# A new table of half steps for the attention phase, sums of exponentials on VectorE for two more batches, and the preparation of w_in2 as one chain with rooms of its own

## The chip, the core and the metric

The kernel runs on one core of a Trainium2 chip. The metric is the device time of one execution in microseconds (us), the median of three runs. TensorE (PE, with its weight loads as PEld), VectorE (DVE), ScalarE (ACT) and SyncE (SP, which only issues DMAs here) each execute their own instructions strictly in the order of the program and wait for each other through semaphores.

## The reference

The inputs are `q`, `k`, `v` of shape (8 batches, 8 heads, 576 tokens, 64) and `phi` (8, 8, 576, 32) in fp32, and the weights of two MLPs, `w_in` (512 x 2048) and `w_out` (2048 x 512), in 64-bit floats.

```python
a = exp(phi - max over tokens); a = a / (sum over tokens + 1e-9)
k_m, v_m = einsum("bhsm,bhsd->bhmd", a, k), einsum("bhsm,bhsd->bhmd", a, v)    # 32 memory slots
scores = q @ k_m^T / sqrt(64); attn = softmax(scores)
x = heads joined (attn @ v_m)                                  # 4608 x 512
y = (s * relu(x @ w_in1) ** 2 + b) @ w_out1                    # first MLP
out = relu(y @ w_in2) ** 2 @ w_out2                            # second MLP
```

## The kernel before

**Arithmetic.** Weights arrive as 64-bit words; `narrow` turns them into fp32 with one ACT and three DVE instructions. Every fp32 operand of a large product is split into a rounded half (an ACT copy) and the remainder (a DVE subtraction), and three products of halves are added (`split3`). The first MLP's second product and both products of the second MLP are done by a scheme with seven products (`e` = 0 to 6) in place of eight, on sums and differences of the quarters of the operands.

**Four stages.** (1) Attention, with the first MLP's hidden layer: the eight batches are taken one after the other. For a batch, `front_max`, `front_t1`, `front_t2`, `front_less` and `front_exp` make the exponentials of phi; `kvs` sums keys and values over the tokens by 72 small matmuls in three groups `g`; it also needs the sum of the exponentials, either by 72 further small matmuls against a column of ones (batches 0 to 2), or by 8 after `front_sum` has added the nine token groups on DVE (batches 3 to 7). `kv_over`, `kv_norm`, `kv_turn` normalize and transpose; `q_turn`, `scores`, `q_exp`, `q_sum`, `p_turn` make the attention weights, in three groups; `fold` multiplies the values into a quarter of `w_in1` (four folds a batch); `hidden` multiplies attention weights with the folded weights. (2) The second product of the first MLP, six blocks of seven products, each in four parts of 12 matmuls of 384 columns. (3) and (4) The two products of the second MLP.

**Half steps.** The attention stage has 256 half steps (slots): batch, 16 blocks of 128 hidden columns, 2 halves of the tokens. Each ends with one `hidden`: six matmuls of 288 columns and an ACT instruction into a tile `r`. After every second slot a DMA writes `r` to DRAM (`rd`). All other work of the attention stage, for this batch and for the next ones, is hung on slots by hand (`on(slot, go, ...)`): it is issued just ahead of that slot's `hidden`. While the stage lasts (`Written.held`), every engine keeps exactly this order, SP's DMAs too. The fold, the scores and the transposes share three PSUM banks (`ps_m`).

**End of the attention stage.** From slot 192 on, and again from 224, `wo1_combos` prepares `w_out1` on ACT and DVE, two steps a slot. The tiles it reads are the four rooms `rc`, in which the first block's `r` is then loaded back (`quad`); the first items of that block (`BEGUN`: square, casts) run in the last slots.

**Second stage.** `block_ready` lists, for each product `e`, what must be ready: squares (ACT), differences (`less`, DVE), casts (`cast`, ACT and DVE, 128 x 768 elements each), and the loads (`quad`). The loop issues them four parts ahead of the matmuls. One step of `win` follows each part: the preparation of `w_in2`, by eight units `u`, 15 steps each: two raw halves are loaded, narrowed, summed, split, and written to DRAM (`wid`), in pairs. Raw halves and results share two rooms of 4 KB a partition (tag `t`).

## Time and profile before

| | us |
|---|---|
| median of three runs (1460.98 to 1464.67) | 1463.64 |
| the profiled execution, its own time | 1464.62 |
| its span, from the first to the last instruction | 1462.8 |
| up to the first `hidden` matmul | 37.1 |
| the 256 half steps | 341.8 |
| second stage (`ya`, `yb`, `yc`) | 362.9 |
| third stage (`pa`, `pb`, `pc`) | 352.3 |
| fourth stage (`qa`, `qb`, `qc`) to the end | 368.8 |

The stages are separated by the first matmul of each. The span leaves out 1.8 us of the execution's own time. In a row of the profile, "idle" is the time in which the engine did nothing before an instruction, and the name behind the arrow is what ended it; "issue" is a wait for nothing that the profile shows. PEclk is the clock that TensorE was granted, as a share of 2.4 GHz.

### The profile page before, as it was taken

The numbers are of one execution on the slowest core, as the hardware profiler recorded it, in microseconds if no ns is written. First come the engines' busy times: TensorE is split into PE (matmuls) and PEld (weight loads), VectorE is DVE, ScalarE is ACT, GpSimd is POOL, SyncE is SP. The second block draws the span as 40 slices with busy tenths as digits, with TensorE's granted clock in tenths as the row PEclk, the third lists the DMA queues.
The fourth block names the chain that finished last, engine by engine and source line by source line (L and its number), as shares of the span: only waits on it lengthen the run. The fifth ranks groups of instructions, "written<-read, shape, count | busy, mean of one in ns | idle before, by whom it ended". The sixth has DMA issues, their size and how long they took to land.

```text
span 1462.8 us, 28453 instructions
## 1 busy us (share of the span) xinstructions
PE 1416.8 (97%) x11616; PEld 1358.4 (93%) x11616; DVE 1068.2 (73%) x1545; ACT 797.6 (55%) x1403; POOL 1.2 (0%) x8
## 2 busy tenths in 40 slices
PE   5899999999899999999999999999999999999998
PEld 3787879878899999999999999999999999999998
DVE  5755777775789989887757786786756677776775
ACT  3555666666777777586535454554434443344443
POOL 0000000000000000000000000000000000000000
PEclk9999999999999999999999999999999999999999
DMA  9977988625574856754696665647796344433441
GB/s 294 285 239 234 291 280 262 220 106 190 173 253 150 306 197 217 234 172 156 231 359 228 246 237 181 247 172 260 277 351 250 113 145 145 143 114 112 138 145 30
DMA packets 207970, 306.47 MB, mean 210 GB/s; under 512 B 48224, under 2 KB 162912, under 8 KB 200288
## 3 DMA queue, kind: packets, MB, share of 16 engines
q1 hardware_dynamic: 207680, 304.39, 62.1%
q8 instruction: 91, 1.49, 0.4%
q14 instruction: 39, 0.32, 0.1%
q10 hardware_dynamic: 160, 0.26, 0.0%
HBM read 180.88 MB, written 123.73 MB: 208 GB/s over the span
## 4 chain that ended last, share of the span: by engine, by line
PE 73%; DVE 12%; DMA 8%; ACT 4%; issue 2%; SPq 1%; ACTq 0%; DVEq 0%
PE qa L109 14%; PE pa L107 13%; PE hps L109 11%; PE qc L109 7%; PE pc L107 7%; PE ya L831 4%; PE qb L109 4%; PE pb L107 3%; DVE rcast L107 3%; DMA wid<-wc 2%; PE yc L831 2%; PE vps L109 2%; PE kvs L109 2%; DMA wt<-in_moe_w_in_dram 2%; DVE wx L107 1%
## 5 line engine op out<-in xcount | busy, mean ns | idle before, releaser
L109 PEld LDWEIGHTS hps<-pt,vp 128*128 128x128 f32 x1536 | 210.4, 190 | 36.7 <-issue 18.3
L109 PE MATMUL hps<-pt,vp 128*128 128x288 f32 x1536 | 234.4, 304 | 6.5 <-ACT r L109 4.3
L109 ACT CAST gc<-h 128x1024 fp32r<-128x1024 f32 x119 | 123.2, 1048 | 174.2 <-DVE h L109 172.6
L109 PE MATMUL qa<-w,gc 128*128 128x256 f32 x1728 | 217.0, 283 | 1.0 <-DVE gc L109 0.7
L109 PEld LDWEIGHTS qa<-w,gc 128*128 128x128 f32 x1728 | 211.5, 192 | 1.6 <-DVE gc L109 1.0
L109 DVE TENSOR_TENSOR gc<-h,gc 128x1024 fp32r<-128x1024 f32 x119 | 145.5, 1224 | 89.0 <-ACT gc L109 89.0
L831 PE MATMUL ya<-rcast,w 128*128 128x384 f32 x1152 | 203.8, 337 | 2.9 <-ACT rcast L107 1.2
L107 PE MATMUL pa<-xc,w 128*128 128x384 f32 x1104 | 204.1, 337 | 0.0
L831 PEld LDWEIGHTS ya<-rcast,w 128*128 128x128 f32 x1152 | 199.8, 188 | 4.4 <-DVE rcast L107 2.1
L107 PEld LDWEIGHTS pa<-xc,w 128*128 128x128 f32 x1104 | 192.8, 188 | 0.6 <-DVE gr L107 0.2
L109 ACT ACTIVATE r<-hps 128x288 f32<-128x288 f32 x256 | 104.1, 416 | 70.0 <-PE hps L109 57.2
L831 PE MATMUL yc<-rcast,w 128*128 128x384 f32 x576 | 106.0, 344 | 5.3 <-DVE rcast L107 5.1
L109 PE MATMUL qc<-w,gc 128*128 128x256 f32 x864 | 109.5, 283 | 0.0
L831 PEld LDWEIGHTS yc<-rcast,w 128*128 128x128 f32 x576 | 103.0, 193 | 6.7 <-DVE rcast L107 6.0
L109 PEld LDWEIGHTS qc<-w,gc 128*128 128x128 f32 x864 | 106.3, 192 | 0.0
L107 PE MATMUL pc<-xc,w 128*128 128x384 f32 x552 | 104.0, 336 | 0.0
L107 PEld LDWEIGHTS pc<-xc,w 128*128 128x128 f32 x552 | 96.6, 188 | 0.3 <-DVE xc L806 0.3
L107 DVE TENSOR_TENSOR rcast<-r,rcast 128x768 fp32r<-128x768 f32 x92 | 84.7, 952 | 16.0 <-ACT rcast L107 16.0
L107 ACT CAST rcast<-r 128x768 fp32r<-128x768 f32 x92 | 73.8, 831 | 16.3 <-DVE r L107 8.5
L107 DVE TENSOR_TENSOR rcast<-rz,rcast 128x768 fp32r<-128x768 f32 x72 | 67.4, 953 | 19.8 <-ACT rcast L107 19.8
L107 ACT ACTIVATE gr<-pa 128x384 f32<-128x384 f32 x46 | 22.6, 492 | 101.1 <-PE pa L107 101.1
L107 DVE SCALAR_TENSOR_TENSOR gr<-gr 128x384 f32<-128x384 f32 x138 | 73.7, 552 | 1.9
(277 smaller groups left out, 1867.2 us busy)
## 6 DMA issues: line engine op xcount, KB each, us to landing
rd<-r SPq DMA_DIRECT2D x128, 288.0 KB, 3.7
gd<-gr SPq DMA_DIRECT2D x96, 384.0 KB, 3.6
h<-gd SPq DMA_DIRECT2D x34, 1024.0 KB, 5.4
wt<-in_moe_w_out_dram SPq DMA_DIRECT2D x16, 1024.0 KB, 6.9
r<-rd SPq DMA_DIRECT2D x16, 768.0 KB, 6.5
wid<-wc SPq DMA_DIRECT2D x24, 512.0 KB, 3.8
rz<-rd SPq DMA_DIRECT2D x16, 768.0 KB, 5.6
kv<-in_k_dram SPq DMA_DIRECT2D x24, 384.0 KB, 6.0
```

The costliest lines, as they stand in the source:

```text
L107: return go(*args, **kwargs)
L109: self.last = go(*args, **kwargs)
L831: nc.tensor.matmul(to[d], lhsT=w[:, wi, d], rhs=cast1[n, e, part][:, u, xi], start=(start and part == 0 and u == 0 and i == 0), stop=(part ...
```

## The change

1. All slots of the attention stage come from a table, `TABLE`, with one entry for each piece of work, in place of a few hand-written tuples and formulas. The start (`"begin"`) is another order too: loads and computing are mixed in it, phi of batch 0 is loaded and its maximum taken in four pieces, `w1_narrow(1, ...)` stands ahead of `kv_turn`, and the two small loads of `s` and `b` move to slots 152 and 153.
2. Batches 0 and 2 get their sum of exponentials from `front_sum`, as batches 3 to 7 do; batch 1 alone keeps the 72 small matmuls.
3. The loads of the first block of the second stage (`"qd"`) and its first items (`"bg"`) move by a few slots; its `b22` is loaded right at the opening of the second stage; in every block, `b12 - b22` and the load of `b21` move from product 4 to the end of product 3 in the list.
4. `prepare_in` takes the place of `combine_in`: one generator over all units, one raw half in the air at a time (one room), two rooms of 2 KB for results, a write to DRAM for each of the seven results (256 KB) in place of pairs (512 KB). A unit has 17 steps; a part takes 1, 0, 1, 2, 1, 1 or 1 of them, by its product.

```diff
+TABLE = {
+    "f": {1: [6, 9, 10, 12, 0], 2: [35, 37, 38, 40, 45], 3: [47, 51, 56, 57, 61], 4: [62, 64, 69, 69, 73], 5: [79, 84, 86, 89, 94], 6: [101, 109, 118,
+        121, 125], 7: [133, 140, 150, 150, 155]},
+    "pt": {1: [26, 30, 32], 2: [62, 63, 63], 3: [81, 87, 92], 4: [110, 115, 123], 5: [139, 148, 155], 6: [167, 176, 188], 7: [201, 208, 223]},
+    "qt": {1: [19, 20, 25], 2: [49, 52, 55], 3: [67, 68, 79], 4: [93, 97, 109], 5: [126, 136, 142], 6: [158, 164, 173], 7: [190, 197, 203]},
+    "kt": {1: 21, 2: 52, 3: 67, 4: 91, 5: 122, 6: 153, 7: 186},
+    "sc": {1: [22, 25, 26], 2: [53, 56, 59], 3: [68, 75, 84], 4: [99, 105, 113], 5: [128, 138, 144], 6: [160, 167, 178], 7: [192, 202, 207]},
+    "ks": {1: [15, 15, 16], 2: [46, 48, 48], 3: [62, 62, 63], 4: [81, 84, 85], 5: [96, 105, 114], 6: [128, 137, 146], 7: [160, 172, 178]},
+    "no": {1: [18, 18, 19], 2: [48, 50, 51], 3: [65, 65, 66], 4: [85, 87, 89], 5: [116, 118, 116], 6: [148, 150, 151], 7: [180, 182, 183]},
+    "ex": {1: [12, 13, 15], 2: [41, 40, 45], 3: [58, 60, 61], 4: [71, 72, 73], 5: [90, 90, 90], 6: [121, 122, 121], 7: [155, 155, 154]},
+    "qe": {1: [24, 27, 28], 2: [54, 58, 59], 3: [69, 80, 85], 4: [102, 107, 115], 5: [130, 138, 146], 6: [162, 171, 180], 7: [193, 204, 209]},
+    "qm": {1: [24, 27, 28], 2: [55, 58, 61], 3: [70, 80, 86], 4: [105, 107, 117], 5: [131, 139, 146], 6: [163, 171, 181], 7: [194, 204, 212]},
+    "fo": {0: [0, 8, 13, 23], 1: [30, 37, 46, 53], 2: [59, 71, 75, 81], 3: [85, 90, 99, 103], 4: [106, 113, 123, 128], 5: [137, 146, 155, 160], 6: [174,
+        178, 183, 191], 7: [199, 215, 212, 223]},
+    "wn": [[0, 0], [3, 3], [8, 9], [10, 11], [15, 16], [17, 18]],
+    "wl": [0, 3, 9, 10],
+    "lq": [1, 8, 4],
+    "lk": [12, 20, 31],
+    "lp": [14, 30],
+    "wo": [[64, 78, 78, 80, 81, 82], [83, 92, 96, 98, 99, 100], [98, 109, 109, 112, 113, 114], [109, 120, 122, 123, 123, 123], [124, 136, 136, 139, 141,
+        141], [138, 148, 151, 152, 153, 162], [152, 164, 167, 168, 171, 171], [164, 176, 178, 179, 185, 186]],
+    "sb": [152, 153],
+    "qd": [225, 227, 240, 244],
+    "begin": [("load_phi", 0), ("load_kv", 0, 2), ("w1_load", 0), ("load_kv", 0, 0), ("load_kv", 0, 1), ("w1_load", 1), ("load_q", 0, 0), ("load_q", 0,
+        1), ("load_q", 0, 2), ("load_phi", 1), ("w1_load", 2), ("front_max", 0), ("front_t1", 0), ("front_t2", 0), ("front_less", 0), ("w1_narrow", 0, 0),
+        ("front_exp", 0, 2), ("w1_load", 3), ("front_exp", 0, 0), ("front_exp", 0, 1), ("w1_narrow", 1, 0), ("kvs", 0, 0), ("front_sum", 0), ("load_kv", 1,
+        0), ("w1_narrow", 0, 1), ("kvs", 0, 1), ("kvs", 0, 2), ("kv_over", 0), ("load_kv", 1, 2), ("kv_norm", 0, 1), ("kv_norm", 0, 0), ("load_kv", 1, 1),
+        ("q_turn", 0, 0), ("w1_narrow", 1, 1), ("kv_turn", 0), ("q_turn", 0, 1), ("scores", 0, 0), ("q_exp", 0, 0), ("scores", 0, 1), ("q_turn", 0, 2),
+        ("q_exp", 0, 1), ("q_sum", 0, 0), ("scores", 0, 2), ("q_exp", 0, 2), ("q_sum", 0, 1), ("p_turn", 0, 0), ("q_sum", 0, 2), ("p_turn", 0, 1), ("fold", 0,
+        0), ("p_turn", 0, 2)],
+    "bg": [242, 245, 248, 250, 252, 253],
+}
...
-    def combine_in(u, pool):
-
-
-        src = w_in2.rearrange("(d p) (h f) -> d p h f", p=P, h=2)[:, :, :, u * P:u * P + P]
-        ts = []
-        for i in range(2):
-            ts.append(pool.tile([P, 1, 512], I64, tag="t", name="wt"))
+    def prepare_in(pool):
+
+
+        def load(u, i):
+            src = w_in2.rearrange("(d p) (h f) -> d p h f", p=P, h=2)[:, :, :, u * P:u * P + P]
+            raw = pool.tile([P, 1, 512], I64, tag="t", name="wt")
             for d in range(2):
-                sp.dma_start(ts[i][:, 0, d * 2 * P:d * 2 * P + 2 * P].rearrange("p (h c) -> p h c", h=2), src[2 * i + d])
-        yield
-        yield
-        x = wst.tile([P, 2, 512], I32, tag="x", name="wx")
-        for i in range(2):
-            for step, _ in enumerate(narrow(ts[i], None, x[:, i:i + 1])):
-                if step == 1:
+                sp.dma_start(raw[:, 0, d * 2 * P:d * 2 * P + 2 * P].rearrange("p (h c) -> p h c", h=2), src[2 * i + d])
+            return raw
+
+        t = load(0, 0)
+        for u in range(NU):
+            yield from (None,) * (3 if u == 0 else 1)
+            x = wst.tile([P, 2, 512], I32, tag="x", name="wx")
+            for i in range(2):
+                for step, _ in enumerate(narrow(t, None, x[:, i:i + 1])):
+                    if step == 0:
+                        yield
+                if i == 0:
+                    t = load(u, 1)
+                    yield from (None,) * 3
+                elif u + 1 < NU:
+                    t = load(u + 1, 0)
+            yield
+            a11, a12, a21, a22 = of_in(x.bitcast(F32))
+            sums_ = wst.tile([P, 4, 2, P], F32, tag="x", name="ws")
+            s1, s2, s4, s3 = [sums_[:, i] for i in range(4)]
+            for out, in0, in1, op in ((s1, a21, a22, ALU.add), (s2, s1, a11, ALU.subtract),
+                                      (s3, a11, a21, ALU.subtract), (s4, a12, s2, ALU.subtract)):
+                with behind():
+                    dve.tensor_tensor(out=out, in0=in0, in1=in1, op=op)
+            yield
+            for e, of in enumerate((a11, s1, s2, s4, s3, a12, a22)):
+                w = pool.tile([P, 2, 2, P], F32R, tag="wc", name="wc", bufs=2)
+                with behind():
+                    act.copy(w[:, 0], of)
+                    dve.tensor_tensor(out=w[:, 1], in0=of, in1=w[:, 0], op=ALU.subtract)
+                sp.dma_start(wid[u][:, e], w.bitcast(F32))
+                yield
+                if e in (1, 4):
                     yield
...
-            sp.dma_start(at["ph", b], pv[b])
+            for part in [slice(n, n + 1) for n in range(NP)] if b == 0 else [slice(NP)]:
+                sp.dma_start(at["ph", b][:, part], pv[b][:, part])
...
-        dve.tensor_reduce(out=pm.rearrange("p (n m) -> p n m", m=M),
-                                in_=at["ph", b].rearrange("p n j m -> p n m j"), axis=AX.X, op=ALU.max)
+        for part in [slice(n, n + 1) for n in range(NP)] if b == 0 else [slice(NP)]:
+            dve.tensor_reduce(out=pm.rearrange("p (n m) -> p n m", m=M)[:, part],
+                              in_=at["ph", b][:, part].rearrange("p n j m -> p n m j"), axis=AX.X, op=ALU.max)
...
-        summed = ([at["es", b]] if g == NJG - 1 else []) if b > 2 else [e[:, :, JG * g + j] for j in range(JG)]
+        summed = ([at["es", b]] if g == NJG - 1 else []) if b != 1 else [e[:, :, JG * g + j] for j in range(JG)]
...
-                if e == 2 and n == 0:
-                    put(None, quad, *b22)
                 if e in (0, 1, 2, 5):
                     put(None, square, (b11, b12, b22, None, None, b21)[e])
-                if e in (1, 2, 4, 6):
-                    put(None, less, *{1: (b11, b12, b11), 2: (b11, b22, b11), 4: (b12, b22, b12), 6: (b21, b21, b11)}[e])
-                if e == 4:
-                    put(None, quad, *b21)
+                if e in (1, 2, 6):
+                    put(None, less, *{1: (b11, b12, b11), 2: (b11, b22, b11), 6: (b21, b21, b11)}[e])
                 if e == 6:
                     put(None, quad, n + 1, "b12", half)
                 for part in (2 * half, 2 * half + 1):
                     put(4 * e + part, cast, e, part, (b11, b11, b11, b22, b12, b21, b21)[e])
+                if e == 3:
+                    put(None, less, b12, b22, b12)
+                    put(None, quad, *b21)
...
-    load_phi(0)
-    w1_load(0)
-    for g in range(NJG):
-        load_kv(0, g)
-    load_q(0, 0)
-    w1_load(1)
-    load_q(0, 1)
-    load_q(0, 2)
-    sp.dma_start(s_sb, s.rearrange("(o n) -> o n", o=1).to_broadcast([P, 1]))
-    sp.dma_start(b_sb, bb.rearrange("(o n) -> o n", o=1).to_broadcast([P, 1]))
-    w1_load(2)
-    w1_load(3)
-    load_phi(1)
-
-    for go, *args in [(front_max, 0), (front_t1, 0), (front_t2, 0), (front_less, 0), (w1_narrow, 0, 0),
-                      (front_exp, 0, 0), (front_exp, 0, 1), (front_exp, 0, 2), (w1_narrow, 0, 1), (kvs, 0, 0),
-                      (kvs, 0, 1), (kvs, 0, 2), (load_kv, 1, 0), (load_kv, 1, 1), (load_kv, 1, 2),
-                      (kv_over, 0), (kv_norm, 0, 0), (kv_norm, 0, 1), (kv_turn, 0),
-                      (q_turn, 0, 0), (scores, 0, 0), (w1_narrow, 1, 0), (q_turn, 0, 1), (q_exp, 0, 0), (w1_narrow, 1, 1),
-                      (scores, 0, 1), (q_turn, 0, 2), (q_exp, 0, 1), (scores, 0, 2), (q_sum, 0, 0), (q_exp, 0, 2),
-                      (q_sum, 0, 1), (p_turn, 0, 0), (q_sum, 0, 2), (p_turn, 0, 1), (fold, 0, 0), (p_turn, 0, 2)]:
-        go(*args)
+    FN = {f.__name__: f for f in (load_phi, w1_load, load_kv, load_q, front_max, front_t1, front_t2, front_less, w1_narrow, front_exp,
+          front_sum, kvs, kv_over, kv_norm, q_turn, kv_turn, scores, q_exp, q_sum, p_turn, fold, wo1_load, wo1_narrow, wo1_sum)}
+    for go, *args in TABLE["begin"]:
+        FN[go](*args)
...
-    fronts = {1: (6, 9, 11, 12, 0), 2: (34, 37, 39, 41, 0), 3: (47, 52, 54, 57, 62), 4: (66, 69, 71, 73, 78),
-              5: (79, 84, 86, 88, 92)}
-    sums_ = {1: (16, 17, 17, 18, 21), 2: (46, 47, 48, 49, 52), 3: (62, 63, 64, 65, 69), 4: (79, 82, 85, 86, 91)}
-    qs = {1: ((19, 20, 23), (22, 23, 25), (26, 28, 30)), 2: ((49, 52, 56), (53, 56, 58), (58, 61, 63)),
-          3: ((66, 68, 77), (73, 76, 82), (80, 86, 92))}
-    folds = {0: (0, 7, 15, 23), 1: (29, 39, 46, 54), 2: (61, 70, 76, 82), 3: (87, 97, 105, 114)}
...
-        y, z = SB * (b - 2), SB * (b - 1)
-        top, turn, back, less, whole = fronts.get(b, (y - 27, y - 18, y - 10, y - 9, y - 3))
-        *adds, norm, last = sums_.get(b, (y, y + 9, y + 18, y + 20, y + 26))
-        qt, sc, pt_ = qs.get(b, ((z - 2, z + 5, z + 13), (z, z + 9, z + 18), (z + 8, z + 17, z + 28)))
...
-            on(folds.get(b, (z + 9, z + 18, z + 26, z + 32))[n], fold, b, n)
...
-    for i, a in zip(range(2, 2 * NV), (0, 2, 8, 10, 15, 17)):
-        on(a, w1_narrow, i, 0)
-        on(a + 1, w1_narrow, i, 1)
...
-        a = 68 + 15 * u
+        a, *steps = TABLE["wo"][u]
         on(a, wo1_load, u)
-        for i, c in enumerate((10, 12, 13, 14, 15)):
-            on(a + c, wo1_narrow, u, i)
+        for i, c in enumerate(steps):
+            on(c, wo1_narrow, u, i)
...
-    for at_, (name, half) in zip((226, 227, 244, 248), (("b11", 0), ("b11", 1), ("b12", 0), ("b12", 1))):
+    for at_, row, of in ((TABLE["sb"][0], s_sb, s), (TABLE["sb"][1], b_sb, bb)):
+        on(at_, sp.dma_start, row, of.rearrange("(o n) -> o n", o=1).to_broadcast([P, 1]))
+    for at_, (name, half) in zip(TABLE["qd"], (("b11", 0), ("b11", 1), ("b12", 0), ("b12", 1))):
...
-    BEGUN = [SB * B - h for h in (10, 9, 8, 6, 5, 3)]
+    BEGUN = TABLE["bg"]
...
-    w64_p = w64x.enter_context(tc.tile_pool(name="w64b", bufs=2, side="right"))
-    win = in_turn([combine_in(u, w64_p) for u in range(NU)])
+    w64_p = w64x.enter_context(tc.tile_pool(name="w64b", bufs=1, side="right"))
+    for half in range(2):
+        quad(0, "b22", half)
+    win = prepare_in(w64_p)
...
-                next(win, None)
+                for _ in range((1, 0, 1, 2, 1, 1, 1)[e]):
+                    next(win, None)
```

## Rows read from the trace of the kernel before

**Rows 1.** Busy time by stage: stretch, length, each engine's busy time (instructions), clock, DMA.
```profile
37.11:378.86 341.75, 326.01 (x4153) 278.25 (x4152) 234.94 (x420) 215.32 (x522) 0.00 (x0) 0.98 0.73 233
378.86:741.71 362.85, 355.14 (x2016) 352.52 (x2017) 304.11 (x388) 250.09 (x330) 0.00 (x0) 0.99 0.64 213
```
**Rows 2.** The chain that ended last: start, length, what, count.
```profile
675.31 16.64 PE ya L831 x96
```
**Rows 3.** Waits of PE, 37 to 379 us: who, for whom, total us, times, longest.
```profile
PE hps L109 <- ACT r L109: 4.3, 5, 2.1
PE vps L109 <- DVE w L109: 1.6, 2, 1.0
```
**Rows 4.** DVE in order of time in the start: start, length, instruction.
```profile
24.79 0.68 DVE L109 TENSOR_SCALAR wx<-wx 128x1024 int32<-128x1024 int32 x1
...
26.76 1.22 DVE L109 SCALAR_TENSOR_TENSOR w<-wt,wx 128x1024 int32<-128x1024 int32 x1
```
**Rows 5.** Groups of instructions by shape, 0 to 380 us: count, busy us, mean ns.
```profile
L109 PE MATMUL kvs<-ones,ph 64*32 64x2 f32 x432 | 6.9, 181 | 2.6 <-issue 2.6
...
L109 PE MATMUL kvs<-ones,es 64*32 64x2 f32 x80 | 1.5, 166 | 0.0
...
L109 DVE TENSOR_REDUCE es<-ph 128x128 f32<-128x1152 f32 x5 | 11.3, 2261 | 0.0
```
**Rows 6.** PE in order of time, batches 0 and 2: start, length, instruction, idle before.
```profile
16.84 0.85 PE L109 MATMUL kvs<-kv,ph 64*32 64x128 f32 x19 [1.87 <-issue]
...
106.69 0.26 PE L109 MATMUL kvs<-ones,ph 64*32 64x2 f32 x13 [0.57 <-issue]
...
112.16 1.06 PE L109 MATMUL hps<-pt,vp 128*128 128x288 f32 x6 [1.19 <-issue]
```
**Rows 7.** DMA queues, 104.4 to 106.7 us: queue, packets, MB, share.
```profile
q8 instruction: 1, 0.02, 2.6%
```
**Rows 8.** PE in order of time, three places of the half steps.
```profile
193.27 1.88 PE L109 MATMUL vps<-w,vmT 64*32 64x512 f32 x18
195.79 1.09 PE L109 MATMUL vps<-w,vmT 64*32 64x512 f32 x14 [0.64 <-DVE vp L109]
...
302.00 1.92 PE L109 MATMUL wsp<-ones,wacc 128*128 128x2 f32 x16 [0.97 <-DVE wacc L109]
...
317.31 1.04 PE L109 MATMUL vps<-w,vmT 64*32 64x512 f32 x2
319.91 1.09 PE L109 MATMUL vps<-w,vmT 64*32 64x512 f32 x14 [1.55 <-DVE pt L109]
```
**Rows 9.** Busy time and granted clock in short stretches, columns as in Rows 1.
```profile
304.40:307.80 3.40, 3.40 (x44) 1.92 (x42) 1.12 (x2) 0.41 (x1) 0.00 (x0) 0.50 0.25 92
...
629.40:632.10 2.70, 0.69 (x4) 0.26 (x2) 2.70 (x4) 2.49 (x6) 0.00 (x0) 0.99 0.49 194
632.10:635.50 3.40, 3.40 (x11) 3.40 (x12) 3.34 (x6) 3.40 (x6) 0.00 (x0) 0.50 0.01 2
```
**Rows 10.** Waits in the second stage, 380 to 640 us.
```profile
ACT wx L107 <- DMA wt<-in_moe_w_in_dram: 15.0, 9, 3.9
ACT rz L107 <- DMA rz<-rd: 11.6, 8, 2.8
...
ACT wc L107 <- DMA wid<-wc: 4.2, 2, 3.3
...
PE yc L831 <- DVE rcast L107: 5.1, 3, 1.9
```
**Rows 11.** DMA issues, 380 to 640 us: count, KB each, median us to landing.
```profile
wid<-wc SPq DMA_DIRECT2D x24, 512.0 KB, 3.8
...
wt<-in_moe_w_in_dram SPq DMA_DIRECT2D x32, 256.0 KB, 3.9
...
wid<-wc SPq DMA_DIRECT2D x7, 256.0 KB, 3.4
```
**Rows 12.** Waits of SP's DMA queue, 0 to 380 us.
```profile
SPq L109 <- ACT w L109: 25.1, 9, 6.5
```

More of the change, by code (lines that the diff above doesn't have):

```diff
@@ L670, in on @@
         events.setdefault(slot, []).append((go, args))
-    fronts = {1: (6, 9, 11, 12, 0), 2: (34, 37, 39, 41, 0), 3: (47, 52, 54, 57, 62), 4: (66, 69, 71, 73, 78),
-              5: (79, 84, 86, 88, 92)}
-    sums_ = {1: (16, 17, 17, 18, 21), 2: (46, 47, 48, 49, 52), 3: (62, 63, 64, 65, 69), 4: (79, 82, 85, 86, 91)}
-    qs = {1: ((19, 20, 23), (22, 23, 25), (26, 28, 30)), 2: ((49, 52, 56), (53, 56, 58), (58, 61, 63)),
-          3: ((66, 68, 77), (73, 76, 82), (80, 86, 92))}
-    folds = {0: (0, 7, 15, 23), 1: (29, 39, 46, 54), 2: (61, 70, 76, 82), 3: (87, 97, 105, 114)}
     for b in range(1, B):
-        y, z = SB * (b - 2), SB * (b - 1)
-        top, turn, back, less, whole = fronts.get(b, (y - 27, y - 18, y - 10, y - 9, y - 3))
-        *adds, norm, last = sums_.get(b, (y, y + 9, y + 18, y + 20, y + 26))
-        qt, sc, pt_ = qs.get(b, ((z - 2, z + 5, z + 13), (z, z + 9, z + 18), (z + 8, z + 17, z + 28)))
+        top, turn, back, less, whole = TABLE["f"][b]
         for g in range(NJG):
-            on(pt_[g], p_turn, b, g)
-            on(qt[g], q_turn, b, g)
+            on(TABLE["pt"][b][g], p_turn, b, g)
+            on(TABLE["qt"][b][g], q_turn, b, g)
         on(turn, front_t1, b)
         on(back, front_t2, b)
-        on(last, kv_turn, b)
+        on(TABLE["kt"][b], kv_turn, b)
         for g in range(NJG):
-            on(sc[g], scores, b, g)
+            on(TABLE["sc"][b][g], scores, b, g)
         for g in range(NJG):
-            on(adds[g], kvs, b, g)
-        for n in range(NV):
-            on(folds.get(b, (z + 9, z + 18, z + 26, z + 32))[n], fold, b, n)
-        on(norm, kv_over, b)
-        on(norm + 1 + (b > 3), kv_norm, b, 0)
-        on(norm + 1 + 2 * (b > 3), kv_norm, b, 1)
+            on(TABLE["ks"][b][g], kvs, b, g)
+        on(TABLE["no"][b][0], kv_over, b)
+        on(TABLE["no"][b][1], kv_norm, b, 0)
+        on(TABLE["no"][b][2], kv_norm, b, 1)
         on(top, front_max, b)
@@ L753, in memory_attention_then_two_relu2_mlps @@
                     turns.remove(turn)
-        if slot == SB * B - 11:
+        if slot == BEGUN[0]:
             begun = block_ready(0)
             ready1.items = lambda n: begun if n == 0 else block_ready(n)
-        if SB * B - 11 <= slot and slot in BEGUN:
+        for _ in range(BEGUN.count(slot)):
             begun.pop(0)[1]()
```

44 lines of the change are left out of this document (14 added, 30 removed).

## The prediction, made before the changed kernel was run

> **What bounds the kernel now.** I read the busy time by stage first. TensorE is the bound in every stage, so a gain can only come from its idle time, from matmuls that go away, or from its clock. The change touches two stretches: the 256 half steps, 341.75 us long with PE busy for 326.01, so 15.7 idle; and the second stage, 362.85 us long [rows 1]. What the second stage would take without loss is seen in the chain that ended last, where 96 of its matmuls run without a gap in 16.64 us, 0.1733 each [rows 2]: 2016 of them are 349.4 us, so 13.4 us are lost there. The third and fourth stages are left as they are.
>
> Next come PE's waits by cause. In the half steps no single cause rules: 4.3 us until ACT had emptied a bank of `hidden`, 1.6 us until DVE had `w_in1` ready for a fold [rows 3], 2.6 us in the small `kvs` matmuls with nothing visible to wait for [rows 5]. The reader is to see that such losses sit at single places, and that each place has a cause in the order of the program. So I went to the order of time at the places where the two tables differ: the start [rows 4], `kvs` [rows 6], folds [rows 8]. Last, the clock [rows 9] and the second stage's waits [rows 10], where DVE comes too late for `yc` (5.1 us), while ACT itself has waited for transfers: 15.0 us for raw `w_in2`, 11.6 for `rz`, 4.2 for its result rooms.
>
> **The change part by part**, as time gained (minus) or lost (plus).
>
> *Start.* Before, DVE does three instructions of `w1_narrow(1, 1)` between the first and the second group's scores, from 24.79 to 27.98, so 3.2 us [rows 4]. The new order puts them ahead of `kv_turn`, where DVE otherwise waits for `kvs` and its normalization. What is late next is the raw weight: its cast stands in ACT's order ahead of `kv_norm`, which waits behind it if the load is late. `front_sum` for batch 0 adds a DVE reduction of 2.26 us (11.3 over 5) [rows 5], issued while DVE waits for keys and values to arrive; it covers it, and without that cover it costs its 2.3. The `kvs` of batch 0 also stands still for 1.87 us [rows 6]; that wait may go with the small matmuls (next part), but the last keys arrive about then. Bounds: all gone, 3.2 + 1.9 = -5.1; nothing gained and the sum on the path, +2.3. I take -2.5, near the one moved piece, since scores, transposes and copies of the next group take part of the room. `w_in1` for the second and third fold of batch 0 is still made by the same chain of DVE instructions from there on, so the 1.6 us of waiting for it [rows 3] stay, shifted as a whole. Loading phi in four pieces and the order of the loads I take at nothing: the total that must arrive before the last group of `kvs` is the same.
>
> *Batch 2's sums.* 432 small matmuls in three batches are busy for 6.9 us, 2.3 a batch; where DVE sums first they are 80 in five batches, 1.5 us, 0.3 a batch [rows 5]: -2.0. DVE's 2.26 are covered, the next `front_max` alone being near. In this batch PE stood for 0.57 and 1.19 us just in or behind these bursts [rows 6], the first while one packet of the instruction queue was under way [rows 7]. No batch that sums on DVE shows such a wait: the 80 have 0.0 idle ahead of them [rows 5]. So -1.8 more. Bounds: -3.8 to 0 (if the waits only move and DVE's sum delays the batch); I take -3.5.
>
> The Trainium skill (Runtime: NRT & Kernel Launch, Instruction fetch mechanics) says that an engine's instructions come in blocks of 256 by a DMA queue of their own while it works on the block before, and calls the cost "mostly hidden". By that, the waits would not be the bursts' doing, and this part and the start would give some 3.6 us less; the rows show the wait and the packet together, so I hold with them for the sum.
>
> *Two folds in one slot.* Slots 105 and 114 each hold two folds, with scores and `kvs`. The 32 matmuls of the first pair last from 193.27 to 196.88, 3.6 us [rows 8]; 14 of the last 16 take 1.09, so two folds without a wait are 2.2. The second fold waits for a bank that DVE has not emptied. The new table has no slot with two folds: -1.4 twice, -2.8. Bounds 0 and -2.8.
>
> *Slot 201.* A fold behind a transpose and the scores in the same or the last slot: from 317.31 to 321.0 instead of 1.1, a loss of 2.6 [rows 8]. The new table has it alone in slot 199, the transpose in 201, the scores in 202. DVE's work on `w_out1` in these slots remains and holds the banks, so I take half, -1.3 (bounds 0, -2.6).
>
> *Slots 191 and 192.* PE waits 0.97 us for the sum of `w_out1` [rows 8], and right behind it the granted clock is 0.50, so 1.2 GHz, for 3.4 us [rows 9], 1.7 us of work. The new table ends that sum two slots earlier: -2.0, bounds 0 and -2.7. A fold now stands in the same slot.
>
> *The rest of the table.* About a hundred further pieces move by a few slots. The idle time not named so far is 15.7 less 1.76, 0.64, 1.55 and 0.97, and less the 2.0 that batch 1 keeps of the 2.6 in [rows 5]: some 9. New crowding stands against it: from slot 58 to 63 DVE gets two `q_sum`, scores, fold, `front_sum`, `front_max`, three `p_turn` before the next batch starts. I bound it by -6 and +6 and take 0.
>
> *End of the half steps.* The 4.3 us until ACT [rows 3] come when `r`'s stores are late: SP stands still, because a load of `quad` waits for a room that ACT still reads for `w_out1` (25.1 us in nine waits [rows 12]). In the new table the second half of `b12` is asked for in slot 244 rather than 248, but the last unit is read until slot 248. SP waits some four slots longer, and all stores of `r` queue behind it; five rooms of `r` cover ten slots. Squares come earlier and more spread, which helps ACT. 0, bounds -3 and +4.
>
> *Second stage.* A part lasts 12 x 0.1733 = 2.08 us. The load of `b21` is issued two parts earlier, 4.2 us more for transfers for which ACT waited at most 2.8 [rows 10]. A raw half has four steps from load to use where both halves had two, 4.2 to 8.3 us against a landing in 3.9 [rows 11], and it waits for DVE alone, not for a store. The load of `b22` goes out first in the stage, but the raw weights now land behind it, and ACT waits for them in order. The new order also asks for no step while the heaviest items (product 2's) are made. PE's wait for DVE is 5.1 us, and behind the last of them (PE busy for 0.69 of 2.70 us) the clock is 0.50 for 3.4 us [rows 9]; the same happens once more in the stage, 2 x 1.7. Half of the 5.1, one clock loss of 1.7, and 1.3 for the start of the stage: -5.5. Bounds: -13.4, all that is lost, and +5.
>
> Against it: a write of 256 KB lands in 3.4 us, one of 512 KB in 3.8 [rows 11], so a smaller write frees its room hardly sooner, and there are twice as many rooms to wait for. That is the last rival.
>
> *Sum.* -2.5 - 3.5 - 2.8 - 1.3 - 2.0 + 0 + 0 - 5.5 = -17.6. The profiled execution took 1464.62 (span 1462.8 and 1.8 outside it), so 1447.0; its time is 1.0 above the median of 1463.64, which gives 1446.
>
> **The rivals.**
> 1. *The table takes away more than the named places.* The rest gives its -6, and the second stage 4 more because both clock losses go: 1436. For it: 9 us of unnamed idle time. Against: DVE's chain early on is not shortened.
> 2. *New crowding eats the gain.* The rest costs +6, the second stage gives 1: 1446 + 6 + 4.5 = 1456.5.
> 3. *PE's waits in `kvs` have another cause than the bursts and stay*, as 0.57, 1.19 and 1.87 elsewhere: 1446 + 3.6 = 1449.6. For it: one of the three ends ahead of a `hidden`, not in a burst [rows 6]. Against: the batches that sum on DVE have none. This is the outcome that the rule quoted above would give.
> 4. *Slower: the result rooms of `prepare_in`.* A room comes back after two or three steps. In product 3, with two steps a part, that is 2.1 to 3.1 us, and the landing alone takes 3.4 [rows 11]. Where ACT waited for such a room before, it was 4.2 us in two waits, 2.1 each [rows 10]. There are 40 reuses (five a unit), and 8 of 28 steps fall there, so 11 of them: 23 us. They reach PE from the point where ACT is more than four parts, 8.3 us, late. Then the time is 1469. Against: most steps are outside product 3, and ACT works for 250.09 of 362.85 us [rows 1].
>
> **How the numbers follow.** Chances: the forecast (1440 to 1452) 0.45, rival 1 0.20, rival 2 0.17, rival 3 0.08, rival 4 0.10. The range from 1434 to 1460 leaves out some 0.06 of rival 1, and 0.13 at the top. A measurement tells about 0.3% apart, 4.4 us, so faster means under 1459.2: 0.45 + 0.20 + 0.08 and two thirds of rival 2, 0.84; same 0.08; slower 0.08.
>
> **What would show it.** First `hidden` at about 34.6 us; no "issue" wait of PE in the `kvs` of batches 0 and 2, while batch 1 keeps one; folds of 1.1 us throughout; no 0.50 clock at the end of the sixth batch; `b22`, `rz` and raw weights waited for less by ACT, its wait for `wid` longer than 4.2. It is wrong if `hidden` waits anew at slot 64 or behind slot 244, or if ACT's waits for `wid` exceed what went.

## The result, and the profile after

The kernel after takes 1449.18 us (median of 4, 1448.45 to 1449.36) against 1462.93 (median of 4 in the same session, 1460.98 to 1464.67): a ratio of 0.9905, 95% interval 0.9888 to 0.9923. That is 13.7 us faster. Forecast were 1446.0, in a range from 1434 to 1460. The profiled executions differ by 15.25 us in span, 1462.83 to 1447.58, and that difference is what is divided up below.

By stretch, busy time and granted clock of the kernel after (length, PE, PE's loads, DVE, ACT, POOL busy, clock, DMA share, GB/s):

```profile
35.17:362.72 327.55, 316.60 (x4025) 272.55 (x4025) 236.90 (x421) 214.23 (x522) 0.00 (x0) 1.00 0.76 245
362.72:727.13 364.41, 355.80 (x2016) 352.30 (x2017) 305.17 (x387) 249.68 (x330) 0.00 (x0) 0.99 0.64 212
```

Against [rows 1] the reader sees at once where the time went. The half steps are 14.20 us shorter, and PE is busy for 9.4 us less in them. The start gave 1.94. The second stage, of which 5.5 us were forecast, is 1.56 us longer. What follows the stage gave 0.7.

PE's waits in the half steps (for whom, total us, times, longest):

```profile
PE vps L143 <- DVE w L143: 2.4, 2, 2.0
PE hps L143 <- ACT r L143: 2.3, 5, 0.9
PE ya L848 <- ACT r L143: 2.3, 1, 2.3
PE hps L143 <- issue: 1.0, 1, 1.0
```

Waiting for ACT to empty `hidden` fell from 4.3 to 2.3 [rows 3], but at the first product of the second stage PE now waits 2.3 us, where it waited 0.5 before. The wait for `w_in1` in batch 0's folds stayed, as forecast, and grew from 1.6 to 2.4 [rows 3]. The one "issue" wait left stands behind batch 1's `kvs`. The sums by small matmuls, by shape (busy us, mean ns, idle ahead): the 432 on single token groups (`ph`) in [rows 5] became 144, and the 80 on sums made by DVE (`es`) became 112.

```profile
L143 PE MATMUL kvs<-ones,es 64*32 64x2 f32 x112 | 2.1, 167 | 0.0
L143 PE MATMUL kvs<-ones,ph 64*32 64x2 f32 x144 | 2.0, 173 | 0.0
```

The folds that [rows 8] showed with waits, in order of time: each is one row of 16 matmuls now, without idle ahead, and so is the sum of `w_out1`. (A row in which the instructions follow each other without idle counts them together: x16.)

```profile
181.80 1.09 PE L143 MATMUL vps<-w,vmT 64*32 64x512 f32 x16
...
187.31 1.09 PE L143 MATMUL vps<-w,vmT 64*32 64x512 f32 x16
...
290.73 1.84 PE L143 MATMUL wsp<-ones,wacc 128*128 128x2 f32 x16
292.50 1.09 PE L143 MATMUL vps<-w,vmT 64*32 64x512 f32 x16
...
301.79 1.09 PE L143 MATMUL vps<-w,vmT 64*32 64x512 f32 x16
```

The second stage's waits of ACT and of PE, against [rows 10]:

```profile
ACT wc L141 <- DMA wid<-wc: 26.4, 15, 4.9
...
ACT rz L141 <- DMA rz<-rd: 10.2, 10, 2.7
...
ACT wx L141 <- DMA wt<-in_moe_w_in_dram: 6.2, 4, 2.3
```

```profile
PE yc L848 <- DVE rcast L141: 4.0, 4, 1.9
PE ya L848 <- DVE rcast L141: 3.8, 4, 1.6
```

The window of [rows 10] ended at 640 us. Over the whole stage before, two of these waits were longer than there:

```profile
ACT rz L107 <- DMA rz<-rd: 13.3, 10, 2.8
...
PE ya L831 <- DVE rcast L107: 1.2, 2, 0.7
```

ACT's wait for raw weights fell from 15.0 to 6.2 us, as meant, and that for `rz` from 13.3 to 10.2; its wait for the result rooms grew from 4.2 to 26.4. PE waits for DVE 7.8 us, where it waited 5.1 for `yc` and 1.2 for `ya` before. Two stretches at a clock of 0.50, so 1.2 GHz, are left in this stage, the first behind a wait of PE of 2.3 us (for ACT, above), the second behind the one of 1.9 for DVE:

```profile
363.60:367.00 3.40, 3.40 (x13) 3.40 (x12) 2.93 (x2) 2.95 (x4) 0.00 (x0) 0.50 0.29 114
554.70:558.10 3.40, 3.40 (x13) 3.40 (x12) 3.08 (x4) 3.40 (x5) 0.00 (x0) 0.51 0.38 142
```

A finer view is the time from the first matmul of `hidden` in one slot to that in another, read from the order of PE's instructions. Here are the two kernels, and three of the runs below (us; y is the first product of the second stage):

| slots | before | after | after again | e3 | e8 |
|---|---|---|---|---|---|
| first `hidden` | 37.11 | 35.17 | 33.42 | 37.37 | 36.91 |
| 0-24 | 40.73 | 38.36 | 38.52 | 40.57 | 41.69 |
| 24-45 | 22.93 | 24.72 | 24.72 | 24.74 | 22.94 |
| 45-50 | 12.16 | 8.32 | 8.32 | 10.41 | 11.98 |
| 50-96 | 69.25 | 66.75 | 66.79 | 66.78 | 69.24 |
| 96-116 | 30.03 | 27.67 | 27.67 | 27.67 | 27.56 |
| 116-184 | 80.56 | 82.85 | 82.84 | 82.82 | 80.58 |
| 184-208 | 34.50 | 29.55 | 29.55 | 29.55 | 31.45 |
| 208-224 | 17.77 | 16.79 | 16.79 | 16.79 | 17.87 |
| 224-y | 33.82 | 32.54 | 32.10 | 32.60 | 32.38 |

From slot 24 to 224 a kernel repeats itself to 0.1 us where the clock doesn't fall, so one edit can be read at its own place to a tenth, far below what two medians tell apart. One slot is an exception: slot 49, where PE waits for nothing visible, took 2.34, 2.06 and 1.79 us in three executions of the old half steps (before, e8, e1). Ahead of slot 24 and behind 224 a kernel doesn't repeat itself so closely.

The two tables don't hang quite the same work on a stretch, so a difference between the kernels there is not all loss or gain. Counted in the two traces, one group's scores and six transposes moved from slots 0 to 24 to slots 24 to 45 (which take 1.8 us more), and one fold each left slots 96 to 116 and 184 to 208 for slots 50 to 96 and 116 to 184 (where 2.3 more are taken); a fold is 1.1 us of PE by the rows above. One group's scores each came into 96 to 116 and 184 to 208, nearly as much. A run below that moves a piece inside one stretch is free of this.

### The profile page after: what moved, and what is told of

Read it like the earlier page. It is cut to its first block, busy times and chain, and to the rows that moved or that the text cites. A ratio compares the mean times of both kernels' runs of the same rounds, so it can differ in the third digit from the quotient of the medians.

```text
span 1447.6 us, 28018 instructions
## 1 busy us (share of the span) xinstructions
PE 1402.8 (97%) x11360; PEld 1347.9 (93%) x11360; DVE 1073.6 (74%) x1550; ACT 796.2 (55%) x1403; POOL 1.2 (0%) x8
## 3 DMA queue, kind: packets, MB, share of 16 engines
q8 instruction: 89, 1.46, 0.4%
## 4 chain that ended last, share of the span: by engine, by line
PE 71%; DVE 11%; DMA 9%; ACT 4%; issue 3%; SPq 1%; ACTq 0%; DVEq 0%
PE qa L143 14%; PE pa L141 13%; PE hps L143 13%; PE qc L143 7%; PE pc L141 7%; PE qb L143 4%; PE ya L848 3%; PE pb L141 3%; DVE rcast L141 3%; DMA wid<-wc 3%; PE vps L143 2%; DMA r<-rd 2%; DMA wt<-in_moe_w_in_dram 2%; DVE r L141 2%; PE sp L143 1%
## 5 line engine op out<-in xcount | busy, mean ns | idle before, releaser
L141 ACT CAST rcast<-rz 128x768 fp32r<-128x768 f32 x72 | 58.7, 834 | 32.4 <-DVE rz L141 15.2
```

The source lines that it names most:

```text
L141: return go(*args, **kwargs)
```

## The experiments

Compared are medians (range), and the ratio to the kernel before in the same session.

| run | time, us | ratio, 95% interval | second stage, us | ACT's wait for `wid` |
|---|---|---|---|---|
| e1 second stage alone | 1463.02 (1461.54-1464.35) | 0.9991 (0.9978-1.0004) | 360.15 | 20.9 |
| e2 table alone | 1448.46 (1447.72-1449.61) | 0.9891 (0.9871-0.9911) | 361.78 | 3.9 |
| e3 batch 2's sum back | 1452.84 (1449.44-1455.78) | 0.9920 (0.9893-0.9946) | 362.30 | 19.7 |
| e4 batch 0's sum back | 1453.82 (1451.70-1454.93) | 0.9925 (0.9905-0.9946) | 364.69 | 24.0 |
| e5 rooms always free | 1447.84 (1444.07-1452.03) | 0.9881 (0.9854-0.9908) | 356.03 | none |
| e6 one step a part | 1449.62 (1447.06-1456.25) | 0.9900 (0.9869-0.9930) | 365.00 | 16.1 |
| e8 three moves alone | 1457.51 (1455.18-1460.90) | 0.9953 (0.9937-0.9969) | 360.97 | 3.0 |
| e9 batch 1 on VectorE | 1446.33 (1441.99-1450.64) | 0.9870 (0.9841-0.9899) | 364.74 | 24.9 |
| e10 small rooms, e9, fold | 1444.14 (1441.85-1450.24) | 0.9878 (0.9857-0.9899) | 359.97 | 3.8 |
| a1 after again | 1449.15 (1444.40-1453.98) | 0.9907 (0.9885-0.9929) | 365.10 | 23.3 |
| e11 old end | 1447.93 (1447.06-1450.62) | 0.9898 (0.9876-0.9920) | 361.29 | 19.8 |
| e12 small rooms, e9 | 1444.42 (1441.07-1445.69) | 0.9869 (0.9844-0.9893) | 356.65 | 3.4 |

**e1 and e2, the two halves.** e1 is the kernel before with `prepare_in`, its pool, its steps and the new order of `b22`, `b21` and `b12`; e2 is the kernel after with all of that put back.

> The kernel before with the second stage's part of the change alone (prepare_in, its rooms and steps, the order of b22, b21 and b12). Theory: the whole gain of 13.7 us lies ahead of the second stage, and there the new waits for wid rooms (20 us of ACT in the kernel after) took the place of those for wt, rz and r; the stage takes 364 us as in the kernel after (362.9 before), the time is 1463 to 1465, no change. Rival: the second stage's change is good for 3 to 5 us, and only the low clock with which the kernel after begins that stage, which comes from how the half steps end there, and what the table leaves behind, ate it: then the stage takes 358 to 360 us here, and the time is 1458 to 1460.

> The kernel after with the second stage of the kernel before (combine_in with two rooms, one step a part, b22 and b21 asked for where they were). Theory: first product y at 362.7 us as in the kernel after, the second stage at 362 to 363 us, and a time of 1447 to 1448, some 1.5 under the kernel after. Rival, as in the run before: the old second stage is slower by 3 to 5 us, 1452 to 1454.

The table alone has the whole gain (1448.46, half a us above its forecast); the second stage's change alone is no change that can be measured: the theory's time held, its 364 us for the stage did not. ACT's waits in e1, then in e2:

```profile
ACT wc L107 <- DMA wid<-wc: 20.9, 14, 4.6
...
ACT wx L107 <- DMA wt<-in_moe_w_in_dram: 7.0, 6, 2.0
```

```profile
ACT wx L141 <- DMA wt<-in_moe_w_in_dram: 15.7, 10, 4.2
...
ACT wc L141 <- DMA wid<-wc: 3.9, 2, 3.5
```

The two waits change places with `prepare_in`, whatever the table is. The stage's length must be read with its low clocks: in a stretch of 3.4 us at 0.50 eleven matmuls begin 0.32 us apart in place of 0.1733 [rows 2, 9], a loss of 1.6. There are two in the stage before, none in e1, one in e2, two in the one after. Without them the stage takes 359.7, 360.2, 360.2 and 361.2 us: the same to 1.5. e1's stage came out at 360.15, 4.3 us below the one after and just beside its rival's 358 to 360; 3.2 us of that is clock, not work.

**e3 and e4, the sums.**

```diff
-        summed = (...) if b != 1 else [...]
+        summed = (...) if b not in (1, 2) else [...]   # e3; e4: if b > 1
```

> The kernel after with batch 2's exponentials summed by TensorE again (72 more kvs pairs of matmuls, 128 in all less 16; front_sum of batch 2 gone), all else at its slot. Theory of the prediction: the small matmuls cost 2.0 us and the waits on instructions in the bursts 1.8, so +3.5 and 1452.7, with PE waits of cause issue back in the kvs of slots 46 to 48. Rival: the 6 us that slots 40 to 64 gave come from the other moves there, and the waits on instructions are hidden: +2.0 or less, 1451.2 or less, no issue wait in these slots.

> The kernel after with batch 0's exponentials summed by TensorE again (front_sum of batch 0 gone), all else where it stands. Theory: the bursts stand on the path that sets the first hidden, with the wait on instructions: first hidden later by 2 to 4 us than 35.17, time 1451 to 1453. Rival: in the start PE waits for keys and values anyway, so the matmuls are hidden and DVE loses 2.3 us of work: first hidden from 33 to 35.2, time 1447 to 1449.2.

From slot 24 on e3 differs in slots 45 to 50 alone, by 2.09 us (the table above): 1.4 in slots 45 and 47, where the matmuls are, and 0.7 behind them in slot 49, where 0.40 can be seen as idle with "issue":

```profile
112.72 1.32 PE L143 MATMUL hps<-pt,vp 128*128 128x288 f32 x8 [0.40 <-issue]
```

Its median is 3.7 above, but its first `hidden` at 37.37 us and a low clock at 57 us, both ahead of the edit, are in that. So the size here is 2.1, near the rival's 2.0, while the wait, which the rival had denied, is real. It stands behind the `kvs`, not in it as the theory had said. That 1452.84 is the theory's 1452.7 is chance.

In e4 PE stops in the third group's burst, and one packet of 16 KB of the instruction queue is under way in that gap (second fence: the queues from 17.3 to 20.75 us, first the loads and stores of the program):

```profile
16.64 0.65 PE L143 MATMUL kvs<-kv,ph 64*32 64x128 f32 x27
20.75 0.86 PE L143 MATMUL kvs<-kv,ph 64*32 64x128 f32 x19 [3.46 <-issue]
```

```profile
q1 hardware_dynamic: 2364, 0.59, 96.4%
q8 instruction: 1, 0.02, 2.4%
```

From the first `kvs` to DVE's first reading of the finished sums it takes 9.65 us (12.64 to 22.29), against 5.38 in the kernel after (14.53 to 19.91), 5.37 in e2 and 5.36 in e3. So batch 0's sum on DVE is worth 4.3 us at its place in this execution, of which 3.46 is the wait. Against the kernel before, where the wait was 1.87 [rows 6], it is 3.1 (8.50, from 9.87 to 18.37). The first `hidden` comes at 37.94, 2.8 later than after, as the theory said, and the time, 1453.82, lies just above its 1451 to 1453. That the packet is the cause of the wait is argued from its place, not tried by itself: the loads took 96.4% of the DMA engines' time in the same gap, and whether a fetch was held up by them, or the burst alone ran ahead of the fetches, no run separates.

**e8, three moves in the kernel before.**

```diff
-... 3: (87, 97, 105, 114)}
+... 3: (87, 97, 103, 112), 7: (199, 210, 218, 224)}
-        for i, c in enumerate((10, 12, 13, 14, 15)):
+        for i, c in enumerate((10, 12, 13, 14, 15) if u < 7 else (10, 11, 12, 12, 13)):
```

> The kernel before with three moves of the change alone: the third and fourth fold of batch 3 in slots 103 and 112 (they shared 105 and 114 with folds of batch 4), the last w_out1 unit's steps ending in slot 186 (188), the first fold of batch 7 in slot 199 (201, with scores). Theory: the stretch of slots 96 to 116 is 2.8 us shorter, 184 to 192 by 2.0 (no low clock there), 200 to 208 by 1.3 to 2.6; time 5 to 7 us under the kernel before, some 1458. Rival: the three places only lose together with the rest of the old table, the waits of DVE's work move on to the next slots, and the time is 1462 to 1464.

Slots 96 to 116 take 2.47 us less, 184 to 208 3.05 less (forecast 2.8 and 3.3), and the other stretches from slot 24 to 224 stay as they were, to 0.2. The 3.05 are 1.67 in slots 184 to 192, where the sum of `w_out1` and the low clock were (the prediction took 2.0), and 1.40 in slots 196 to 208, where the fold of slot 201 was (1.3). The median, 8 us under that of the kernel before in the same session, is better than forecast. PE at the end of the sixth batch, and the clock where [rows 9] had 0.50:

```profile
300.04 1.84 PE L109 MATMUL wsp<-ones,wacc 128*128 128x2 f32 x16
303.56 1.09 PE L109 MATMUL vps<-w,vmT 64*32 64x512 f32 x16
```

```profile
304.40:307.80 3.40, 3.40 (x32) 3.22 (x25) 2.83 (x7) 2.69 (x7) 0.00 (x0) 1.00 0.15 58
```

In the old table the three places are worth 5.5 us, and the rival, that they only lose together with the rest of it, is out.

**e5 and e6, the rooms.** e5 stores other data, so that no store holds a room; e6 spreads the steps.

```diff
-                sp.dma_start(wid[u][:, e], w.bitcast(F32))
+                sp.dma_start(wid[u][:, e], weight("one", u, e).bitcast(F32))   # e5
-                for _ in range((1, 0, 1, 2, 1, 1, 1)[e]):
+                for _ in range((1, 1, 1, 1, 1, 1, 1)[e]):   # e6
```

> The kernel after, but the stores to wid take pieces of the prepared w_out1, which lie ready, in place of the rooms wc, so that a room is free as soon as VectorE has written it and no store waits for VectorE. The traffic is the same; the product with w_in2 is not the reference's. Theory: ACT's waits for wid rooms (26 us in 15) go, and with them most of PE's waits of 10.6 us in the second stage: 5 us or less left, the stage at 357 to 360 us (364.4), the time 1443 to 1446. Rival: the heavy items at the start of products 1 and 6 (squares and differences) set PE's waits whatever the rooms do: 9 to 10 us stay, 1448 to 1450.

> The kernel after with one step of prepare_in in every part, product 1 and product 3 as well (after: none and two). Theory, by the working of the last rival: rooms come back too early where two steps fall in a part; ACT's wait for wid falls from 26 us to 10 or so, PE's waits in the stage from 10.6 to 7, time 1446 to 1448. Rival: product 1 is where the heaviest items are made, and a step there adds to PE's waits 2 to 4 us: 1451 to 1453.

e5's second stage, and PE's waits in it:

```profile
365.58:721.61 356.03, 352.27 (x2016) 350.68 (x2017) 304.88 (x387) 250.85 (x330) 0.00 (x0) 1.00 0.58 193
```

```profile
PE ya L848 <- ACT r L143: 2.8, 1, 2.8
PE ya L848 <- DVE rcast L141: 2.0, 2, 1.0
PE yc L848 <- DVE rcast L141: 1.8, 3, 1.3
```

With the rooms free the stage is 8.4 us shorter, and PE waits 3.8 us for DVE in place of 7.8. Some 1.6 of the 8.4 are a stretch at low clock fewer. The theory held in the stage, but not in all: PE's waits are 6.6 us with that at the first product, where 5 or less were forecast, and the median of 1447.84 lies above 1443 to 1446. (The profiled execution, at 1444.07, is the fastest of four; the others have no trace.) That the rooms were held by the stores, and little by DVE's writing, is seen in ACT's wait for a room that DVE has yet to write: 3.0 us in all of e5's stage. The edit also frees SP's queue from waiting for DVE ahead of each store, so its share is not separated from the rooms'; e12 does that.

In e6 neither side held: with one step in each part the wait for `wid` falls only to 16.1 us, that for raw weights rises to 12.1, and nothing is won. The two steps of product 3 were not the cause. Counted in the order of the program, only 2 of the 15 waits of the kernel after, 2.9 of the 26.4 us, fall on pieces made in product 3; 9.4 us in three waits fall in product 6. The longest, on ACT, with the DMA queues and the landing of the stores in the stretch where two of them were under way (536.9 to 544.7 us), then in one without loads (550.5 to 556.7):

```profile
544.71 0.41 ACT L141 CAST wc<-ws 128x256 fp32r<-128x256 f32 x1 [4.88 <-DMA wid<-wc]
```

```profile
q1 hardware_dynamic: 3240, 2.63, 102.3%
...
wid<-wc SPq DMA_DIRECT2D x2, 256.0 KB, 7.6
```

```profile
q1 hardware_dynamic: 432, 0.79, 33.9%
...
wid<-wc SPq DMA_DIRECT2D x4, 256.0 KB, 2.0
```

The same store lands in 7.6 us while the next block's `b12` and `b22`, asked for in product 6, are loaded, and in 2.0 us without loads; the median is 3.8. So two rooms are too few not for a piece every 2 us as such, but where landings are long. This is read from one trace; no run moves the loads.

**e9, e10 and e12, what could be won.** The store of a piece needs a room only for its high part, if the low part is written in place:

```diff
-            for e, of in enumerate((a11, s1, s2, s4, s3, a12, a22)):
-                w = pool.tile([P, 2, 2, P], F32R, tag="wc", name="wc", bufs=2)
+            for e, of in ((0, a11), (5, a12), (6, a22), (1, s1), (2, s2), (3, s4), (4, s3)):
+                w = pool.tile([P, 2, P], F32R, tag="wc", name="wc", bufs=4)
...
-                    dve.tensor_tensor(out=w[:, 1], in0=of, in1=w[:, 0], op=ALU.subtract)
-                sp.dma_start(wid[u][:, e], w.bitcast(F32))
+                    dve.tensor_tensor(out=of.bitcast(F32R), in0=of, in1=w, op=ALU.subtract)
+                sp.dma_start(wid[u][:, e, 0], w.bitcast(F32))
+                sp.dma_start(wid[u][:, e, 1], of)
```

> The kernel after with batch 1's exponentials summed by VectorE first as well (front_sum of batch 1 in slot 15). Theory: 1.4 us of small matmuls and the 1.0 us that PE stands behind them with no visible cause go, and DVE has cover: 1446 to 1447. Rival: DVE's 2.3 us delay the chain that makes w_in1 for the folds of slots 12 and 23, and the last kvs group waits for the sum: 1449 to 1451.

> The kernel after with three edits. First, of each prepared piece of w_in2 only the high part gets a room (half the size, so four of them); the low part is written in place over the piece and stored from there. Second, batch 1 is summed by VectorE as in the run before. Third, the third fold of batch 0 goes from slot 13 to 15 (PE stands 3.5 us there for w_in1). Theory: ACT's wait for wid falls from 26 us to under 8 and the stage to 357 to 360 us; batch 1 gives 2.4; the fold gives 1 to 2: 1439 to 1443. Rival: twice as many stores, of 128 KB in pieces of 512 B a partition on the low side, keep SP's queue and the rooms of x and ws busy, so that ACT waits for those as long: stage 363 to 366, and the fold only moves the wait to slot 15: 1446 to 1448.

> The run with small rooms for w_in2 and batch 1 summed by VectorE, with the third fold of batch 0 back in slot 13. Theory: the fold's move gave nothing (the wait went to kvs), so 1443 to 1445, with the second stage at 360 us again. Rival: the earlier 1444.1 owed 1 to 2 us to the fold: 1445 to 1447.

e12's second stage, and ACT's waits in it:

```profile
359.31:715.96 356.65, 353.50 (x2017) 352.11 (x2017) 304.98 (x387) 249.84 (x330) 0.00 (x0) 0.99 0.66 217
```

```profile
ACT wx L141 <- DMA wt<-in_moe_w_in_dram: 11.5, 5, 5.5
...
ACT wc L141 <- DMA wid<-wc: 3.4, 4, 1.6
```

Here SP still waits for DVE ahead of the stores of low parts (23.0 us in 23 waits for the sums `ws` alone), and the stage is as short as in e5: the rooms were the cause. Of ACT's waits for transfers the one for raw weights (11.5 us) is now the largest, and little of it reaches PE, whose waits in the stage behind the first product are

```profile
PE yc L849 <- DVE rcast L141: 1.9, 1, 1.9
PE yc L849 <- ACT rcast L141: 1.2, 1, 1.2
```

The size is less sure than the cause: the same code for this stage took 359.97 us in e10, with 5.4 us of such waits and with 6.8 us at low clock like e12. Batch 1 on VectorE gives 2.2 to 2.3 us in slots 0 to 24, read where the clock does not fall there (36.18 in e12; 38.36 and 38.52 in the kernel after) (forecast for e9 were 2.4). The fold's move cost more than it gave: in e10 the wait went to `kvs`,

```profile
PE kvs L143 <- ACT ph L143: 3.5, 2, 2.9
```

and slots 0 to 24 take 37.67 there, 1.5 more than in e12. So e10 stayed above its forecast of 1439 to 1443, by 1 us. Against the kernel after in the same session e10 is 5.0 us faster (1444.14 against 1449.15, medians of six whose ranges overlap). e12 ran in another session; its ratio to the kernel before is 0.9869, against 0.9907 for the kernel after, with intervals that just overlap.

**e11, the end of the half steps.** `qd` is [226, 227, 244, 248] and `bg` [246, 247, 248, 250, 251, 253] again.

> The kernel after with the old end of the half steps: the four loads of b11 and b12 asked for in slots 226, 227, 244, 248 (after: 225, 227, 240, 244) and the six first items of the second stage in slots 246 to 253 (242 to 253). Theory of the prediction: 0, the stores of r are late either way; slots 240 to 255 change by less than 1 us against 15.2. Rival: the new end gave 1 to 2 us in slots 240 to 255, but left 1.8 us of waiting at the first product of the second stage and the low clock behind it (1.7 us): then slots 240 to 255 take 16.4 us again, the wait at the first product shrinks to under 1 us, no low clock begins there, and the time is the same or up to 2 us better, 1447 to 1449.

Slots 240 to 255 take 16.30 us (15.19 after), and the wait at the first product is 0.5 us in place of 2.3. From slot 240 to the second stage it is 17.8 against 18.4: the new end is worth nothing, or -0.6. The low clock did not go; it begins at 356.5, behind a wait of PE of 1.46 us and a short one between slots 249 and 251. The rival held but for that, and the theory did not: its slots 240 to 255 change by 1.1, not by less than 1.

**a1, the kernel after again.**

> The kernel after, unchanged, on the same chip: how far the start and the second stage differ from execution to execution. Every theory expects 1448 to 1450, the same time of every slot behind slot 16 to 0.1 us up to slot 224, and a second stage of 361 to 365 us, according to how often the clock falls in it.

It held in all but the second stage, 365.10, by 0.1.

## Why the prediction was right, and which term was mis-sized

| term | forecast | in the two profiles | by experiment |
|---|---|---|---|
| start | -2.5 | -1.9 | first `hidden` at 33.4 to 37.4 (median 34.3) in ten executions with the new order, 36.9 to 37.1 in three with the old |
| batch 2's sums (slots 45-50) | -3.5 | -3.8 | 2.1 the sums (e3), 1.7 the new order there |
| two folds in a slot | -2.8 | -2.4 | -2.5 (e8) |
| slots 184-208 | -3.3 | -4.95 | -3.05 (e8) |
| rest of the table and its end | 0 | -3.05 | end 0 to +0.6 (e11) |
| second stage | -5.5 | +1.6 | 0 to +1.5, low clocks left out (e1, e2) |
| stages behind | 0 | -0.7 | |
| sum | -17.6 | -15.2 | |

**What was right.** That PE is the bound, that the loss sits at single places, and that each place has its cause in the order of the program: 11.1 of the half steps' 14.2 us lie in the slots named, and the runs that change the named causes alone give 7.6 of them (2.1 in e3, 2.5 and 3.05 in e8). Folds, the sum of `w_out1` with its clock and batch 0's sum stood up one by one.

**What was luck.** The total is near because two errors cancel. The second stage came out 7.1 us worse than forecast; the half steps gave 4.6 more than the named parts, and the stages behind, which have no part in the change, 0.7.

**The term that failed is the second stage.** The working had both sides of it: the raw weights' wait falls, and the last rival, with 11 reuses at 2 us, prices ACT's new wait at 23 us. Measured are 26.4 in 15, and 20.9 and 23.3 in e1 and a1. What was wrong is that I gave this price to a rival at 0.10 and left it out of the forecast, although one edit brings both. By the prediction's own sign the term is refuted: ACT's waits for `wid` grew by 22.2 us, while those for raw weights and `rz` lost 8.8 and 3.1. That the price was right to some 15% is luck in part, for the rival looked for the waits in product 3, where hardly any are. And it was wrong in how they would reach PE. It added 23 us to what was there, where they mostly *took the place* of the raw weights' waits and PE's own waits for DVE only went from 6.3 to 7.8 us. Hence neither -5.5 nor the rival's +17.5 (23 less 5.5), but nothing. That gains of this size were to be had in the stage is shown by e12, 6.2 us under the kernel before with as much low clock, and less surely by e10, 2.9 under it.

**Batch 2's sums** came out at the right size for a reason that was half right. e3 brings back 0.7 of the 1.76 us of waits, not all; the other 1.1 went with the new order of slots 45 to 50. Why is not shown; the wait in slot 49 also differs by 0.5 us between executions of the same code. The Trainium skill (Runtime: NRT & Kernel Launch, Instruction fetch mechanics) calls the cost of crossing from one block of instructions to the next "mostly hidden". If the packet is the cause, the row of e4 does not agree for bursts of such small matmuls: 3.46 us with a packet under way.

**The start** was right in size, but the load order, which I took at nothing, was not nothing. ACT and PE in the start of the kernel before, then of the kernel after, in order of time:

```profile
9.29 0.99 ACT L109 ACTIVATE ph<-ph 128x384 f32<-128x384 f32 x2 [0.81 <-DVE ph L109]
9.87 1.54 PE L109 MATMUL kvs<-kv,ph 64*32 64x128 f32 x48 [1.20 <-ACT ph L109]
```

```profile
12.35 1.12 ACT L143 ACTIVATE wx<-wt 128x1024 f32<-128x1024 f32 x1 [10.34 <-DMA wt<-in_moe_w_in_dram]
13.37 1.33 ACT L143 ACTIVATE ph<-ph 128x384 f32<-128x384 f32 x3
14.53 1.53 PE L143 MATMUL kvs<-kv,ph 64*32 64x128 f32 x48 [7.17 <-DMA kv<-in_v_dram]
```

The exponentials of batch 0 stand behind ACT's first step on a raw weight, which waits 10.34 us for its load, so they begin at 13.37 us; before, they began at 9.29. The first `kvs` waits for the values' load besides, and begins 4.7 us later than before. Two gains outweigh this: from the first `kvs` to the finished sums it takes 3.1 us less (5.38 against 8.50), and from there to the first `hidden` 3.5 less (15.26 against 18.74), where the prediction had DVE's moved instructions at 3.2. So the forecast had the two gains at 5.1 at most and took half of that for another reason; they gave 6.6, the loads took 4.7 back, and the -1.9 was met by luck. An earlier load was not tried.

**The rest**, -3.05 of the -6 to +6, includes a low clock at 65 us that all three executions with the old table show; of 11 with the new one, 6 show one that begins between 52 and 58 us and 5, the kernel after among them, none (1.2 to 2.2 us of slots 0 to 24). The measured 1449.18 stands at rival 3's 1449.6 by accident: its mechanism, waits that stay, is not what the traces show.

## What to carry to other kernels

When a change removes one wait and brings in another on the same engine, price both and put the difference into the forecast; a rival that keeps only one of them is no case at all. A room that goes out by a store is busy for the landing, not for the compute: count rooms by the landing time where the queue is full, not by its median, and make the room smaller before spreading the steps. Where the order of a program is fixed, read an edit from its own slots: most repeat to 0.1 us, where the times of the kernel after ranged over 0.9 us in one session and 9.6 in another.

## What the runs showed of the hardware that was not expected

The granted clock falls to 0.50 (1.2 GHz) for 3.4 or 6.8 us, in e4 once for 10.3 (from 19.7), and not each time behind the same wait: at the first product of the second stage PE waited 2.3 and 2.2 us in the kernel after and in a1, and the clock fell, and 2.1 and 2.2 in e10 and e12, and it did not. Identical code differs in it: of seven executions with the same program up to slot 24 (after, a1, e2, e3, e5, e6, e11), four show a low clock that begins between 52 and 58 us and three none. With the same start the first `hidden` came at 33.42 to 37.37 us in ten executions. The loads explain 2.2 of that (first `kvs` at 12.74 to 14.97); the stretch from the sums to the first `hidden` gives the rest (15.3 to 17.3, longest in e9 and e3, which have a low clock there at 21.8 and 22.9 for 6.8). The wait for nothing visible grew to 3.46 us in one burst, the largest of all seen.
